# Program order from a list scheduler, first loads in 512-byte pieces, sink rows packed into 32

## The chip, the cores and the metric

The kernel runs on one core of a Trainium2 chip. The metric is the device time of one execution in microseconds (us). A core has five engines that each run their own instructions strictly in program order: PE (matrix products; its weight loads are shown as PEld), DVE (vector work), ACT (activation functions and copies), POOL (here mostly a DMA issuer that also casts in flight) and SP (issues DMAs only). Engines wait for one another by semaphores; an instruction that waits holds up everything behind it on its engine.

## The reference, cut to what matters

```python
# q, k, v: batch 4, heads 8, seq 768, head_dim 64; n_sink 4, window 128
scores = scale * q @ k.T                      # keep: is_sink | (0 <= row - col < window)
a = softmax(where(keep, scores, -1e9));  x = a @ v      # x as 3072 tokens x 512
h = x @ w_in                                  # 512 -> 2048
P = a0 + a1*h + a2*h**2 + a3*h**3
Q = 1 + |b0|*|h| + |b1|*h**2
out = (P / (Q + 1e-6)) @ w_out                # 2048 -> 512
```

Attention with a window of 128 and four sink tokens, then two matrix products with a rational function between them.

## The kernel before

The 3072 tokens are cut into 12 steps of 256 (three per batch entry). A step's attention runs per head pair i (four of them): `scores` (four products into the one buffer ps_s), `exps` on ACT, `mask` on DVE for two pairs at a time, `attend` on PE into the one buffer ps_m, `normalize` on DVE. `sink_scores` and `sink_exps` treat the sink tokens once per step; `spread_k` lays the transposed k out as block-diagonal weights. `turn_x` transposes the result: by PE for steps 0 and 1, by SP's DMA transposes afterwards.

The second half of a step m works on h as 128 partitions x 4096 columns. `project_in` makes it in four quarters (16 products each, into two buffers ps_h), `copy_in` moves a quarter to SBUF on ACT. DVE then does `magnitude` (|h|), a half of `square`, `denominator`, `even`, `odd`, `odd_h`, `numerator`; ACT does the other half of `square`, and the reciprocal of Q as `log_den` (Ln) and `recip_den` (Exp). `gate` on DVE multiplies, `project_out` (two tiles of tokens, each in two groups of eight products, one buffer ps_out) and `store` finish.

What sets the order: the program is written out by hand. A prologue does step 0's attention, then a loop over slots t (L611 ff.) issues in each slot a quarter of `project_in`, an attention pair two steps ahead, one group of `project_out`, and the element-wise work by j = t mod 4. Every engine's order follows from that. Data arrive by three ways: SP loads step 0's k, q and v as fp32, which are cast on ACT and DVE; POOL's DMAs load everything later with a cast; SP's DMA transposes turn k and q from step 2 on. POOL has eight DMAs under way at most: the ninth waits until the first has landed.

Of the kernel before, what the change touches and what calls it, by code (L numbers as in the profile page):

```python
# [17 lines left out]
def kernel(  # L18
# [62 lines left out]
    k_sink = [const_pool.tile([P, 640], BF16, name=f"k_sink_{n}") for n in range(2)]  # L81
# [12 lines left out]
    one_eps = const_pool.tile([P, 1], FP32, name="one_eps")  # L94

# [13 lines left out]

    def load_q(tile_i):  # L110
# [42 lines left out]
    def cast_v():
        for e in range(2):
            lo, hi = e * 64, (e + 1) * 64
            nc.vector.tensor_copy(out=v_bd[0][lo:hi, :, :, e, 0:D], in_=raw["v"][lo:hi])

    def load_w_in(half):
        f0, f1 = half * DF // 2, (half + 1) * DF // 2
        for c in range(NDMC):  # L160
            nc.gpsimd.dma_start(out=w_in_sb[c][:, f0:f1], in_=moe_w_in[c * P:(c + 1) * P, f0:f1])

    def load_w_out(part):
        for c in range(part * NFFC // 2, (part + 1) * NFFC // 2):
            nc.gpsimd.dma_start(out=w_out_sb[c], in_=moe_w_out[c * P:(c + 1) * P, :])
# [576 lines left out]
```

## Time and profile before

| | us |
|---|---|
| median of 3 runs (297.49 to 298.47) | 298.21 |
| profiled execution, its own time | 298.49 |
| its span, first to last instruction | 296.8 |
| DVE busy in the span | 239.3 |
| PE busy | 235.5 |
| ACT busy | 214.2 |
| POOL busy (issuing DMAs counts) | 116.1 |

How to read it: three engines are busy for more than 70% of the span, DVE most. These shares are means over stages; the windows in the rows below cut the span at the end of step 0's attention, the start of the first `gate` and the end of the last one.

### The profile page before, as it was taken

What the parts mean: (1) busy time and instruction counts of PE and PEld (TensorE: products, weight loads), DVE (VectorE), ACT (ScalarE), POOL (GpSimd) and SP (SyncE); (2) the same over time, 40 slices, a digit from 0 to 9 for tenths busy, and PEclk for the clock granted to TensorE, in tenths of its full rate; (3) what the DMA queues carried; (4) which work ended last, traced back from release to release, by engine and by line L of the source; (5) the groups of instructions that cost most, each with busy time, mean ns of one, the idle gap of its engine ahead of it and who ended that gap; (6) DMA issues with size and microseconds to landing.
All of it is one profiled execution on the core that took longest, in us unless ns stands there. A gap on an engine that the chain in (4) does not pass through costs nothing.

```text
span 296.8 us, 4876 instructions
## 1 busy us (share of the span) xinstructions
PE 235.5 (79%) x1856; PEld 167.4 (56%) x1876; DVE 239.3 (81%) x320; ACT 214.2 (72%) x201; POOL 116.1 (39%) x178
## 2 busy tenths in 40 slices
PE   0516866658609899999989899998999999997864
PEld 0414555546507777767767677676677767652321
DVE  6606623736794999999999999999999999999930
ACT  2104261684735998989979899898998989897810
POOL 8938668879091046181651793380000000000000
PEclk9999997996957999999999999999999999997999
DMA  8999999999999199398995999292110121100111
GB/s 160 127 171 80 157 127 158 142 171 201 143 114 47 29 129 128 80 136 108 116 103 105 147 107 121 27 140 63 55 41 17 53 55 53 38 35 35 71 38 72
DMA packets 116632, 28.94 MB, mean 98 GB/s; under 512 B 110464, under 2 KB 112512, under 8 KB 116608
## 3 DMA queue, kind: packets, MB, share of 16 engines
q0 software_dynamic: 72752, 12.74, 64.1%
q1 hardware_dynamic: 43856, 15.88, 26.6%
q8 instruction: 15, 0.25, 0.4%
q14 instruction: 9, 0.07, 0.1%
HBM read 27.30 MB, written 6.29 MB: 113 GB/s over the span
## 4 chain that ended last, share of the span: by engine, by line
DVE 56%; PE 16%; DMA 8%; ACT 7%; issue 6%; SPq 5%; POOL 1%; DVEq 0%; ACTq 0%; POOLq 0%
DVE sq L470 8%; DVE num L474 8%; PE ps_h L419 7%; DVE g L492 6%; DVE den L454 6%; DVE x_n L384 5%; DVE num L460 4%; DVE den L449 4%; DVE e L348 4%; PE ps_out L500 4%; DVE sq L443 3%; PE ps_o L371 3%; DMA b_bc<-in_moe_b_dram 3%; DVE sq L465 2%; ACT hb L426 2%
## 5 line engine op out<-in xcount | busy, mean ns | idle before, releaser
L419 PE MATMUL ps_h<-xblk,w_in_sb 128*128 128x256 bf16 x768 | 98.5, 284 | 8.3 <-DMA xblk<-x_n 7.5
L500 PE MATMUL ps_out<-w_out_sb,g 128*128 128x512 bf16 x364 | 87.8, 385 | 7.6 <-ACT o_t L505 4.0
L419 PEld LDWEIGHTS <-w_in_sb 128*128 128x128 bf16 x768 | 76.4, 102 | 20.5 <-DMA xblk<-x_n 7.8
L151 POOL DMA_DIRECT2D v_bd<-in_v_dram x88 | 57.3, 670 | 28.7 <-PE ps_o L371 12.2
L426 ACT ACTIVATE hb<-ps_h 128x1024 bf16<-128x1024 f32 x48 | 49.1, 1022 | 26.2 <-PE ps_h L419 26.2
L500 PEld LDWEIGHTS <-g 128*128 128x128 bf16 x384 | 37.3, 99 | 45.6 <-issue 7.0
L480 ACT ACTIVATE lnq<-den,one_eps,qsc 128x2048 f32<-128x2048 bf16 x24 | 50.4, 2098 | 10.9 <-DVE den L454 10.9
L486 ACT ACTIVATE den<-lnq 128x2048 bf16<-128x2048 f32 x24 | 46.2, 1924 | 0.0
L341 ACT ACTIVATE e<-ps_s 128x768 bf16<-128x768 f32 x48 | 38.9, 816 | 2.8 <-PE ps_s L331 2.8
L131 POOL DMA_DIRECT2D k_bf<-in_k_dram x22 | 20.3, 937 | 46.9 <-DMA kT_flat<-k_bf 46.6
L371 PE MATMUL ps_o<-v_bd,e 128*128 128x130 bf16 x352 | 31.4, 228 | 9.1 <-DVE x_n L384 4.2
L331 PE MATMUL ps_s<-qT,kT 128*128 128x192 bf16 x192 | 25.7, 260 | 14.9 <-ACT e L341 14.6
L371 PEld LDWEIGHTS <-e 128*128 128x128 bf16 x352 | 26.1, 102 | 19.4 <-DVE x_n L384 4.9
L454 DVE TENSOR_TENSOR den<-den,sq 128x2048 bf16<-128x2048 bf16 x24 | 29.0, 1215 | 0.0
L331 PEld LDWEIGHTS <-kT 128*128 128x128 bf16 x192 | 18.4, 104 | 17.7 <-issue 16.2
L474 DVE TENSOR_TENSOR num<-num,sq 128x4096 bf16<-128x4096 bf16 x12 | 27.5, 2292 | 0.4
L492 DVE TENSOR_TENSOR g<-num,den 128x4096 bf16<-128x4096 bf16 x12 | 27.4, 2284 | 0.1
L470 DVE TENSOR_TENSOR sq<-sq,hb 128x4096 bf16<-128x4096 bf16 x12 | 27.4, 2284 | 0.1
L384 DVE SCALAR_TENSOR_TENSOR x_n<-ps_o,csc,rec 128x256 bf16<-128x256 f32 x48 | 23.2, 484 | 1.7
L381 DVE RECIPROCAL rec<-ps_o 128x4 f32<-128x4 f32 x48 | 8.5, 177 | 18.7 <-PE ps_o L371 18.5
L348 DVE TENSOR_TENSOR e<-e,edge 128x1024 bf16<-128x1024 bf16 x24 | 16.4, 683 | 8.3 <-ACT e L341 8.3
L441 ACT ACTIVATE sq<-hb 128x2048 bf16<-128x2048 bf16 x12 | 22.9, 1910 | 0.0
(67 smaller groups left out, 205.8 us busy)
## 6 DMA issues: line engine op xcount, KB each, us to landing
out_dram<-o_t SPq DMA_DIRECT2D x24, 256.0 KB, 2.4
k_bf<-in_k_dram POOLq DMA_DIRECT2D x22, 128.0 KB, 5.4
v_bd<-in_v_dram POOLq DMA_DIRECT2D x88, 32.0 KB, 4.4
q_bf<-in_q_dram POOLq DMA_DIRECT2D x21, 128.0 KB, 5.9
w_in_sb<-in_moe_w_in_dram POOLq DMA_DIRECT2D x8, 256.0 KB, 7.6
w_out_sb<-in_moe_w_out_dram POOLq DMA_DIRECT2D x16, 128.0 KB, 5.0
stage_q<-in_q_dram SPq DMA_DIRECT2D x3, 256.0 KB, 5.2
xblk<-x_n SPq DMA_TRANSPOSE x40, 3.5
```

The source lines that it names most:

```text
L151: nc.gpsimd.dma_start(out=t_[lo:hi, i, :, e, 0:D], in_=src)
L331: nc.tensor.matmul(ps[:, n // 2, (n % 2) * 192:(n % 2) * 192 + 192], lhsT=kT_fix[s % 2][:, i * NHF + n, :], rhs=qT_fix[b % 2][:, i, c:c + ...
L371: nc.tensor.matmul(ps_o[:, n, :], lhsT=l_, rhs=r_.rearrange("p e c -> p (e c)"), start=(m == 0), stop=(m == len(terms) - 1))
L419: nc.tensor.matmul(ps[:, n, :], lhsT=w_in_sb[c][:, fc * P:(fc + 1) * P], rhs=xblk[m][:, c, :], start=(c == 0), stop=(c == NDMC - 1))
L426: nc.scalar.activation(out=hb[m][:, j * GW:(j + 1) * GW], in_=ps_h.pop((m, j)).rearrange("p n c -> p (n c)"), func=AF.Copy)
L454: nc.vector.tensor_tensor(out=den[m][:, c], in0=den[m][:, c], in1=sq[m][:, c], op=ALU.add)
L470: nc.vector.tensor_tensor(out=sq[m][:, c], in0=sq[m][:, c], in1=hb[m][:, c], op=ALU.mult)
L474: nc.vector.tensor_tensor(out=num[m][:, c], in0=num[m][:, c], in1=sq[m][:, c], op=ALU.add)
L480: nc.scalar.activation(out=lnq[m, part], in_=den[m][:, c], func=AF.Ln, scale=qsc, bias=one_eps)
L486: nc.scalar.activation(out=den[m][:, c], in_=lnq[m, part], func=AF.Exp, scale=-1.0)
L492: nc.vector.tensor_tensor(out=g_of[m][:, c], in0=num[m][:, c], in1=den[m][:, c], op=ALU.mult)
L500: nc.tensor.matmul(ps_out[m, tt], lhsT=g_of[m][:, co:co + P], rhs=w_out_sb[fc], start=(fc == 0), stop=(fc == NFFC - 1))
```

## The change

The hand-written prologue and slot loop go. Every unit of work becomes a piece with an engine, an assumed length, a rank and the pieces that it depends on. At build time a list scheduler goes through simulated time: whenever an engine is free it takes, of the pieces whose inputs are done and whose PSUM buffer is free, the one with the lowest rank. The order in which pieces were taken is the order in which the program is then emitted. The chip sees the same five in-order engines; the work per step is unchanged.

Beside the order: k and q of step 0 (256 tokens) are loaded with two neighbouring tokens per partition, so that a piece of memory is 512 bytes and not 256, and the casts and the copies after the transposes sort even and odd tokens again (those of q move from DVE to ACT); v of step 0 comes through POOL with the cast in flight and not through SP; the sink rows of v are loaded densely into 32 partitions and spread by DVE (once per batch entry) and not by eight small DMAs; b and a are loaded right behind k and q; and the second half of w_in is issued in front of k and q of step 1.

```diff
-    k_sink = [const_pool.tile([P, 640], BF16, name=f"k_sink_{n}") for n in range(2)]
+    KW = P + 2 * NS
+    k_sink = [const_pool.tile([P, NPB * KW], BF16, name=f"k_sink_{n}") for n in range(2)]
...
+    def load_two(dst, src):
+        nc.sync.dma_start(out=dst.rearrange("p (h t d) -> p h t d", h=H, t=2),
+                          in_=src[:, 0:2 * P, :].rearrange("h (p t) d -> p h t d", t=2))
+
+    def by_token(t_):
+        return t_.rearrange("p (h t d) -> p t h d", h=H, t=2)
...
+    def cast_k2():
+        k_bf[0] = early[:, 3:5, :]
+        nc.vector.tensor_copy(out=k_bf[0].rearrange("p t (h d) -> p t h d", h=H),
+                              in_=by_token(raw["k"]))
...
+    def load_v_sink():
+        for b in range(B):
+            nc.gpsimd.dma_start(out=stage_s[:, b, :], in_=v[b, :, 0:NS, :])
+
+    def spread_v_sink(b):
+        nc.vector.tensor_tensor(
+            out=v_sink[0:NR, b, :, 0:D], in0=stage_s[:, b:b + 1, :].to_broadcast([NR, H, D]),
+            in1=ind[0:NR].unsqueeze(2).to_broadcast([NR, H, D]), op=ALU.mult)
+        nc.vector.tensor_copy(out=v_sink[0:NR, b, :, D], in_=ind[0:NR])
...
+    def place_q2():
+        dst = qT_fix[0][:, :, 0:2 * P].rearrange("p i (c t) -> p i c t", t=2)
+        for t in range(2):
+            nc.scalar.activation(out=dst[:, :, :, t], in_=ps_q["two"][:, :, t, :], func=AF.Copy)
...
+            if s == 0:
+                for t in range(2):
+                    nc.vector.tensor_copy(
+                        out=kT[lo:hi, :, lo:hi].rearrange(
+                            "p (i n) (c t) -> p i n c t", i=NPB, t=2)[:, :, :, :, t],
+                        in_=src[lo:hi, :, t, :].rearrange("p i (n c) -> p i n c", n=NHF))
...
-    cast_k()
-    turn_k(0)
-    spread_k(0)
-    for n in range(NQ_HW):
-        cast_q(n)
-        turn_q(n)
-    sink_edge, csc, qsc, (a0, a1, a2, a3) = scalars()
-    load_w_in(0)
-    feed(1)
-    load_v(1)
-    load_w_in(1)
...
-    for t in range(NSLOT + 14):
-        p, j = divmod(t, 4)
-        in_m = p < NSTEP
-        ns = ahead_s.get(t, (t + 8,))
...
-        if j == 1:
-            if in_c:
-                log_den(c, A_)
-                denominator(c, B_)
-            if in_g:
-                gate(c - 1)
...
+    piece(("load_k2",), "SP", 0.6, -22, load_k2, kind="hw", load=2.0)
+    piece(("load_q2",), "SP", 0.6, -21, load_q2, kind="hw", load=2.0)
+    piece(("load_q", 2), "SP", 0.6, -20, lambda: load_q(2), kind="hw", load=1.4)
...
+    for half in range(2):
+        for c in range(NDMC):
+            piece(("load_w_in", half, c), "POOL", 0.55, -18.9 + half * 0.05,
+                  lambda half=half, c=c: load_w_in(half, c), kind="sw", load=1.25)
...
+    piece(("scal_in",), "SP", 1.0, -19.8, lambda: (
+        nc.sync.dma_start(out=b_bc, in_=moe_b.partition_broadcast(P)),
+        nc.sync.dma_start(out=a_bc, in_=moe_a.partition_broadcast(P))), kind="hw", load=0.2)
+    piece(("babs",), "ACT", 0.15, -12, lambda: nc.scalar.activation(out=babs, in_=b_bc, func=AF.Abs),
+          [("scal_in",)])
...
+    for b in range(B):
+        piece(("spread_vs", b), "DVE", 0.7, -18 if b == 0 else 12 * b - 13,
+              lambda b=b: spread_v_sink(b),
+              [("consts",), ("clear_vs",), ("load_vs",), ("norm", 0, NPB - 1) if b else None])
...
+            piece(("exp", m, hf), "ACT", on_act(HW), r_ + 7.2 + hf,
+                  lambda m=m, part=part: recip_den(m, part), [("ln", m, hf)])
+        piece(("even", m), "DVE", 1.27, r_ + 6.2, lambda m=m: even(m),
+              [("sq", m, 0), ("sq", m, 1), ("gate", m - 1) if m else ("cast_q",)])
...
+        piece(("gate", m), "DVE", on_dve(MW, 2), r_ + 9.3, lambda m=m: gate(m),
+              [("num", m), ("exp", m, 0), ("exp", m, 1)]
+              + ([("gemm2", m - 2, NTS - 1, 1)] if m >= 2 else
+                 [("turned_k", 0), ("turn_q2",), ("turn_q", 2)]))
...
+                able = [w for w in waiting[e]
+                        if (not w.takes or room[w.takes])
+                        and (not w.kind or lanes[w.kind][count[w.kind] % 8] <= now + 1e-9)]
+                if not able:
+                    continue
+                w = min(able, key=lambda w_: (w_.rank, w_.order))
+
+                if any(f_.eng == e and left[f_.name] == 1 and f_.rank < w.rank - HOLD_R
+                       for end, x_ in ends if end < now + HOLD_F * w.length
...
+                if w.takes:
+                    room[w.takes] -= 1
+                if w.frees:
+                    returns.append((end, w.frees))
+                ends.append((end, w))
+                done.append(w)
+            if not moved:
...
+    for w in run_list():
+        if w.run:
+            w.run()
```

Where the instructions stand now, at three places. First ACT, from the first quarters of h (hb) on; e are the exps of the pairs, lnq is `log_den`, sq is ACT's half of `square`, xblk the copy behind `turn_x`. Before:

```order
L404 ACTIVATE xblk<-ps_xT 128x512 x2
L426 ACTIVATE hb<-ps_h 128x1024 x2
L341 ACTIVATE e_1_95<-ps_s 128x4x192
L318 ACTIVATE e_sink<-ps_sink 128x256
L341 ACTIVATE e_1_95<-ps_s 128x4x192
L426 ACTIVATE hb<-ps_h 128x1024
L341 ACTIVATE e_1_97<-ps_s 128x4x192 x2
L404 ACTIVATE xblk<-ps_xT 128x512
L426 ACTIVATE hb<-ps_h 128x1024
L441 ACTIVATE sq<-hb 128x2048
```

The same place now:

```order
L437 ACTIVATE xblk<-ps_xT 128x512 x2
L462 ACTIVATE hb<-ps_h 128x1024 x2
L477 ACTIVATE sq<-hb 128x2048
L462 ACTIVATE hb<-ps_h 128x1024
L516 ACTIVATE lnq<-den,one_eps,qsc 128x2048
L375 ACTIVATE e_1_95<-ps_s 128x4x192
L347 ACTIVATE e_sink<-ps_sink 128x256
L375 ACTIVATE e_1_95<-ps_s 128x4x192
L462 ACTIVATE hb<-ps_h 128x1024
L375 ACTIVATE e_1_97<-ps_s 128x4x192
L522 ACTIVATE den<-lnq 128x2048
```

The square and the first logarithm of step 0 moved in front of step 1's first exps, and the fourth quarter of h stands in front of step 1's third exps and no longer behind all four and the first `turn_x`.

Second DVE, around a `gate` (g) in the middle of the program; num<-num,sq is `numerator`, num<-sq `even`, den<-hb `magnitude`, den<-den,sq `denominator`, rec and x_n are `normalize`, e is `mask`. Before:

```order
L474 TENSOR_TENSOR num<-num,sq 128x4096
L381 RECIPROCAL rec<-ps_o 128x4
L384 SCALAR_TENSOR_TENSOR x_n<-ps_o,csc,rec 128x2x128
L348 TENSOR_TENSOR e_1_97<-e_1_97,edge 128x16x64
L449 TENSOR_SCALAR den<-hb 128x1024
L443 TENSOR_TENSOR sq<-hb 128x2048
L454 TENSOR_TENSOR den<-den,sq 128x2048
L381 RECIPROCAL rec<-ps_o 128x4
L384 SCALAR_TENSOR_TENSOR x_n<-ps_o,csc,rec 128x2x128
L454 TENSOR_TENSOR den<-den,sq 128x2048
L492 TENSOR_TENSOR g<-num,den 128x4096
```

Now:

```order
L496 TENSOR_SCALAR num<-sq,acoef 128x4096
L501 TENSOR_SCALAR sq<-sq,acoef 128x4096
L416 RECIPROCAL rec<-ps_o 128x4
L419 SCALAR_TENSOR_TENSOR x_n<-ps_o,csc,rec 128x2x128
L506 TENSOR_TENSOR sq<-sq,hb 128x4096
L510 TENSOR_TENSOR num<-num,sq 128x4096
L416 RECIPROCAL rec<-ps_o 128x4
L419 SCALAR_TENSOR_TENSOR x_n<-ps_o,csc,rec 128x2x128
L382 TENSOR_TENSOR e_1_95<-e_1_95,edge 128x16x64
L485 TENSOR_SCALAR den<-hb 128x1024
L528 TENSOR_TENSOR g<-num,den 128x4096
L490 TENSOR_TENSOR den<-den,sq 128x2048
```

Before, the two denominators of step m+1 stood between the numerator and the gate of step m; now the gate stands in front of both. The denominator rows of step m itself stand one row (of `spread_k`) and this whole stretch ahead of its gate.

Third POOL, from its first DMAs on. Before:

```order
L206 DMA v_sink<-in_v_dram 4x4x64 x8
L161 DMA w_in_sb_105<-in_moe_w_in_dram 128x1024
L161 DMA w_in_sb_106<-in_moe_w_in_dram 128x1024
L161 DMA w_in_sb_107<-in_moe_w_in_dram 128x1024
L161 DMA w_in_sb_108<-in_moe_w_in_dram 128x1024
L131 DMA k_bf<-in_k_dram 128x8x64 x2
L118 DMA q_bf<-in_q_dram 128x8x64 x2
L151 DMA v_bd_92<-in_v_dram 64x4x64 x8
```

Now:

```order
L170 DMA v_bd_91<-in_v_dram 64x4x64 x8
L195 DMA stage_s<-in_v_dram 32x1x64 x4
L176 DMA w_in_sb_105<-in_moe_w_in_dram 128x1024
L176 DMA w_in_sb_106<-in_moe_w_in_dram 128x1024
L176 DMA w_in_sb_107<-in_moe_w_in_dram 128x1024
L176 DMA w_in_sb_108<-in_moe_w_in_dram 128x1024
L176 DMA w_in_sb_105<-in_moe_w_in_dram 128x1024
L176 DMA w_in_sb_106<-in_moe_w_in_dram 128x1024
L176 DMA w_in_sb_107<-in_moe_w_in_dram 128x1024
L176 DMA w_in_sb_108<-in_moe_w_in_dram 128x1024
L162 DMA k_bf<-in_k_dram 128x8x64 x2
L136 DMA q_bf<-in_q_dram 128x8x64 x2
```

k and q of step 1 moved behind all of w_in.

## Rows read from the trace of the kernel before

**Rows 1.** Four windows: length, busy PE, PEld, DVE, ACT, POOL; clock, DMA share, GB/s.
```profile
0.00:30.85 30.85, 10.52 (x74) 7.91 (x74) 16.83 (x50) 6.94 (x11) 22.98 (x47) 1.00 1.12 133
30.85:95.19 64.34, 41.05 (x353) 32.86 (x354) 35.97 (x66) 33.62 (x35) 42.79 (x61) 0.84 1.77 143
95.19:284.92 189.73, 176.68 (x1399) 123.60 (x1417) 186.53 (x207) 172.43 (x154) 50.33 (x71) 0.99 0.63 79
284.92:296.80 11.88, 7.24 (x32) 3.04 (x32) 0.00 (x0) 1.19 (x2) 0.00 (x0) 1.00 0.15 56
```
**Rows 2.** Timeline of the start: start, length, instruction, idle before it and releaser.
```profile
12.94 0.52 PE L331 MATMUL ps_s<-qT,kT 128*128 128x192 bf16 x2
...
21.54 0.20 ACT L234 ACTIVATE babs<-b_bc 128x2 f32<-128x2 f32 x1 [11.43 <-DMA b_bc<-in_moe_b_dram]
...
31.99 3.08 PE L419 MATMUL ps_h<-xblk,w_in_sb 128*128 128x256 bf16 x14 [0.26 <-ACT xblk L404]
...
36.47 1.91 PE L419 MATMUL ps_h<-xblk,w_in_sb 128*128 128x256 bf16 x16
```
**Rows 3.** The chain that ended last: start, length, what (a DMA to its landing).
```profile
12.22 9.29 DMA b_bc<-in_moe_b_dram
```
**Rows 4.** Groups by line on DVE in the start: count, busy, mean ns, idle.
```profile
L156 DVE CAST v_bd<-stage_kv 64x1024 bf16<-64x1024 f32 x2 | 1.4, 689 | 0.0
L293 DVE COPY kT<-ps_kT 64x1024 bf16<-64x1024 bf16 x4 | 2.7, 686 | 0.8 <-PE ps_kT L278 0.8
L263 DVE COPY qT<-ps_qT 128x512 bf16<-128x512 bf16 x5 | 2.1, 424 | 2.9 <-PE ps_qT L262 2.9
```
**Rows 5.** Timeline of POOL: issues of step 1's v, and what each waited for.
```profile
19.46 0.61 POOL L151 DMA_DIRECT2D v_bd<-in_v_dram x1 [0.72 <-DMA w_in_sb<-in_moe_w_in_dram]
21.12 0.61 POOL L151 DMA_DIRECT2D v_bd<-in_v_dram x1 [1.06 <-DMA w_in_sb<-in_moe_w_in_dram]
22.41 0.61 POOL L151 DMA_DIRECT2D v_bd<-in_v_dram x1 [0.67 <-DMA k_bf<-in_k_dram]
23.93 1.98 POOL L151 DMA_DIRECT2D v_bd<-in_v_dram x3 [0.91 <-DMA k_bf<-in_k_dram]
```
**Rows 6.** DMA issues by line: count, KB, median us to landing.
```profile
qT<-q_bf SPq DMA_TRANSPOSE x19, 3.5
v_sink<-in_v_dram POOLq DMA_DIRECT2D x8, 2.0 KB, 3.9
```
**Rows 7.** Groups by line on DVE, whole span.
```profile
L454 DVE TENSOR_TENSOR den<-den,sq 128x2048 bf16<-128x2048 bf16 x24 | 29.0, 1215 | 0.0
L474 DVE TENSOR_TENSOR num<-num,sq 128x4096 bf16<-128x4096 bf16 x12 | 27.5, 2292 | 0.4
L470 DVE TENSOR_TENSOR sq<-sq,hb 128x4096 bf16<-128x4096 bf16 x12 | 27.4, 2284 | 0.1
L384 DVE SCALAR_TENSOR_TENSOR x_n<-ps_o,csc,rec 128x256 bf16<-128x256 f32 x48 | 23.2, 484 | 1.7
L449 DVE TENSOR_SCALAR den<-hb 128x1024 uint32<-128x1024 uint32 x24 | 18.1, 754 | 0.0
L348 DVE TENSOR_TENSOR e<-e,edge 128x1024 bf16<-128x1024 bf16 x24 | 16.4, 683 | 8.3 <-ACT e L341 8.3
L460 DVE TENSOR_SCALAR num<-sq,acoef 128x4096 bf16<-128x4096 bf16 x12 | 16.1, 1344 | 0.2
```
**Rows 8.** Groups by line on ACT, whole span.
```profile
L480 ACT ACTIVATE lnq<-den,one_eps,qsc 128x2048 f32<-128x2048 bf16 x24 | 50.4, 2098 | 10.9 <-DVE den L454 10.9
L426 ACT ACTIVATE hb<-ps_h 128x1024 bf16<-128x1024 f32 x48 | 49.1, 1022 | 26.2 <-PE ps_h L419 26.2
L486 ACT ACTIVATE den<-lnq 128x2048 bf16<-128x2048 f32 x24 | 46.2, 1924 | 0.0
L341 ACT ACTIVATE e<-ps_s 128x768 bf16<-128x768 f32 x48 | 38.9, 816 | 2.8 <-PE ps_s L331 2.8
L505 ACT ACTIVATE o_t<-ps_out 128x512 f32<-128x512 f32 x24 | 14.4, 599 | 11.2 <-PE ps_out L500 11.2
```

More of the change, by code (lines that the diff above doesn't have):

```diff
@@ L153, in cast_v, with cast_q @@
[L153 to L158, printed above, removed]
-        f0, f1 = half * DF // 2, (half + 1) * DF // 2
[L160 to L165, printed above, removed]
+    def cast_q():
+        nc.scalar.activation(out=early[:, 2, :], in_=raw["q"][:, 2, :], func=AF.Copy)
@@ L251, in scalars, with turn_q2 @@
         nc.vector.tensor_tensor(out=acoef[:, 1:4], in0=a_bc[:, 1:4], in1=cpow, op=ALU.mult)
-        return sink_edge, csc, qsc, [acoef[:, n:n + 1] for n in range(4)]
+    kT_flat, ps_q, ps_x = {}, {}, {}
+    def turn_q2():
+        ps = ps_op.tile([P, 512], FP32, tag="ps_out", name="ps_qT").bitcast(BF16)
+        ps = ps.rearrange("p (i t c) -> p i t c", i=NPB, t=2)
+        for i in range(NPB):
+            for t in range(2):
+                nc.tensor.transpose(ps[:, i, t, :], early[:, t, i * P:(i + 1) * P], ident)
+        ps_q["two"] = ps
@@ L538, in do_scores @@
-    def do_scores(n):
-        s, i = divmod(n, NPB)
-        if s < NSTEP:
-            scores(s, i)
-            exps(s, i)
-    def do_mask(n):
-        s, i = divmod(n, NPB)
-        if s < NSTEP and i % 2 == 1:
-            mask(s, i // 2)
-    def do_attend(n):
-        s, i = divmod(n, NPB)
-        if s < NSTEP:
-            attend(s, i)
-    def do_norm(n):
-        s, i = divmod(n, NPB)
-        if s < NSTEP:
-            normalize(s, i)
-            if i % 2 == 1:
-                turn_x(s, i // 2)
@@ new lines, with piece, on_dve @@
+    work = {}
+    class Piece:
+        pass
+    def piece(name, eng, length, rank, run, after=(), takes=None, frees=None, lat=0.0, kind=None,
+              load=0.0):
+        w = Piece()
+        w.name, w.eng, w.length, w.rank, w.run = name, eng, length, rank, run
+        w.after = [a_ for a_ in after if a_ is not None]
+        w.takes, w.frees, w.lat, w.kind, w.load = takes, frees, lat, kind, load
+        w.order = len(work)
+        assert name not in work
+        work[name] = w
+    def on_dve(cols, rate, extra=0.0):
+        return 0.065 + extra + cols / (960.0 * rate)
@@ new lines @@
+    piece(("babs",), "ACT", 0.15, -12, lambda: nc.scalar.activation(out=babs, in_=b_bc, func=AF.Abs),
+          [("scal_in",)])
+    piece(("scalars",), "DVE", 1.7, -12, scalars, [("babs",)])
+    piece(("mask_tiles",), "DVE", 1.4, -17, mask_tiles, [("consts",)])
+    for n in range(3):
+        piece(("clear_v", n), "DVE", 1.0, (-20, -10, -4)[n], lambda n=n: zero(v_flat[n]))
+        piece(("ones", n), "DVE", 0.2, (-20, -10, -4)[n], lambda n=n: ones_columns(v_fix[n]),
+              [("clear_v", n)])
@@ new lines @@
+    for n in range(2):
+        later = [("norm", 0, NPB - 1)] if n else []
+        piece(("clear_kT", n), "DVE", 0.95, -19.9 + n * 5, lambda n=n: zero(kT_fix[n]))
+        piece(("clear_ks", n), "DVE", 0.35, -19.8 + n * 12, lambda n=n: zero(k_sink[n]), later)
+        piece(("clear_qT", n), "DVE", 0.3, -19.8 + n * 12,
+              lambda n=n: nc.vector.memset(qT_fix[n][:, :, S:S + P], 0.0), later)
+        for grp in range(2):
+            piece(("clear_e", grp, n), "DVE", 0.35, -19.7 + n * 5,
+                  lambda grp=grp, n=n: zero_gaps(e_fix[grp, n]))
```

603 lines of the change are left out of this document (326 added, 277 removed).

## The prediction, made before the changed kernel had run

> **What bounds the kernel now.** I read the windows first, cut at the end of step 0's last `normalize` (30.85), the start of the first `gate` (95.19) and the end of the last one (284.92). In the third window DVE is busy 186.5 of 189.7 us: it waits 3.2 us in all, so there DVE is the bound, with PE behind it (176.7 busy, 13.0 idle) [rows 1]. The last 11.9 us are without DVE: two `project_out` tiles, copy, store. In the first two windows DVE works only 16.8 of 30.9 and 36.0 of 64.3 us. The column adds up to 239.3 us of work; of its idle time 14.0 + 28.4 = 42.4 us lie ahead of the first gate. That is what an order can win here; 239.3 plus the tail is what it can't pass.
>
> Then the timeline, for what those 42.4 us wait for. In the start, ACT's first exps stand behind `babs`, which needs b; b is issued at 12.22 behind eight loads of v and lands 9.29 later [rows 3], so ACT idles 11.43 and goes on at 21.54 [rows 2], though the first scores ran at 12.94. In the second window PE is busy 41 us, ACT 34 and DVE 36 of 64, at a granted clock of 0.84 [rows 1]: none is full, they wait for each other in turn, since the slots mix quarters of h with attention of steps 1 to 3 in one fixed order.
>
> **The start, part by part.** b now goes out as SP's fourth load, some 8 us earlier. The exps then hang on q: its casts, transposes and copies take the same time as before, moved from DVE to ACT, and the first scores stay at about 13. So exps begin at about 13.3 instead of 21.7. From there to the last `normalize` it took 9.2 us before; that gives 22.5. DVE's own list gives nearly the same: POOL issues eight v and four sink loads (0.6 us each, from 3.6 on) until 11, the sink rows land 3.9 later [rows 6], and behind the spread that waits for them stand two clears, two masks and four `normalize`: 22.8. I take 22.8, 8 us earlier. Bounds: 20 (the sink rows in time, all clears hidden) to 31 (nothing won).
>
> [...]
>
> Work added or removed on DVE: the cast of v goes (2 x 0.69), three copies of q go to ACT (3 x 0.42), the spread of step 0's k is four strided copies instead of two of 0.69 [rows 4]. No row shows a copy with step 2; below lies half a row each (0.34), above the fp32 rate of `normalize` (0.484 for 256 elements, 0.97 for 512 [rows 7]); I take the 0.42 of the other PSUM copy, 1.7 in all, and keep 1.4 to 3.9. The four spreads of sink rows (512 elements each on 32 partitions) lie between 0.34 and 1.1, I take 0.75, 3.0 in all. Sum: -1.4 - 1.3 + 0.3 + 3.0 = +0.7, so 240.0 us of DVE work; -1 to +4 with the bounds.
>
> [...]
>
> The 512-byte loads and the wider casts save at most the wait for k and q, and DVE is still at its clears then: 0, bounds -1.5 to +1 (the strided casts at up to twice 0.84).
>
> **The fill, from 22.8 to the first gate.** `turn_x` and its copy as before: 31.99 - 30.85 = 1.1 [rows 2], so the first quarter of h starts at 23.9; 3.1 and 1.9 us for two quarters [rows 2], one copy of 1.0 [rows 8]: 29.9. DVE has only the other three spreads and two clears there.
>
> k and q of step 1 now stand behind all of w_in. Tiles of w_in landed 1.66 us apart, tiles of k 1.5 [rows 5]. Eight from 11.5 on: 25.5; four of k and q: 31.5. Before, they had landed by about 25 but were first used behind the first quarter of h, after 32, so this costs little: PE turns k at 29.7, q 4 at 33.
>
> ACT then has, from 29.9, the square (as long as an Exp, 1.9), the third copy once its quarter is there (34.0), the first logarithm 2.1, two exps of 0.82 and the small sink one [rows 8]: the first mask of step 1 at 38.1. From that mask to the gate DVE has 4 masks, 2 `magnitude`, 7 `normalize` (0.18 + 0.48), one square and one denominator, 2 spreads, `even` and `odd`, `odd_h`, `numerator`: 2.7 + 1.5 + 4.6 + 2.4 + 1.9 + 2.7 + 2.3 + 2.3 = 20.4 us [rows 4, 7]. One wait inside: PE does the third `attend` of step 1 behind the first scores of step 2, which need q 6. That lands behind eight v (0.61 each) and four tiles of 1.5: 42.9, plus a transpose of 1.2 + 3.5 [rows 6] = 47.6; DVE wants that `attend` at 44.8 and gets it at 49.3: 4.5 us. So the first gate starts at 38.1 + 20.4 + 4.5 = 63.0. Bounds: 55 (no such wait, w_in faster) to 80 (the fill's 28.4 us of idle time unchanged).
>
> **From the first gate to the end.** At that gate the new order has done less: before, 52.8 us of DVE work lay ahead of it. Of that the new order still has to do four `normalize` (2.6), two masks (1.4), a spread and a sink mask (1.0), one `magnitude`, one square and two denominators of step 1 (4.4): 9.4. With the +0.7 that is 44.1 us done, 195.9 left. Idle time in the rest: I keep 3.2, since DVE's work per step is the same and PE has the same share of it (176.7 plus some 9 us for two more quarters and four more pairs, in 199 us: 93%, as before). Tail 11.9, the same instructions.
>
> Sum: 63.0 + 195.9 + 3.2 + 11.9 = 274.0 us of span. The profiled execution took 1.7 us more than its span (298.49 against 296.8) and the median of the runs lay 0.3 below it: 275.4 us.
>
> **The rivals.** *The loads set the fill.* For it: the DMA share is 1.77 in the second window, and w_in's second half, some 7 us, now goes ahead of step 1. If the fill keeps its idle time: 240.0 + (42.4 - 8) + 3.2 + 11.9 = 289.5, 290.9 us measured. Against it: before, the waits there are mostly of engine for engine.
>
> *PE and DVE hold each other up in the steady part.* ps_m and ps_s are single, PE has 7% to spare, and the order comes from assumed lengths. One us more per step and 11 steps: 286.4. Against: units as long as now and no new dependence.
>
> *Slower.* Place: the gate. Before, it stands behind the next step's two denominators, nearly a step after its own. Now only `even`, `odd`, `odd_h`, `numerator`, two `normalize`, a mask and a `magnitude` lie between the second denominator and its gate: 2.7 + 2.3 + 2.3 + 1.3 + 0.7 + 0.75 = 10.0 us [rows 7]. In that time ACT must do Ln 2.1 and Exp 1.9 and what is queued between them; the longest such list of the new order has a copy of h, a sink exp, an exp, a square and an output copy: 1.0 + 0.3 + 0.8 + 1.9 + 0.6, in all 8.6 [rows 8]. The margin is 1.4. It decides once ACT's list, waits for PE included, exceeds 10.0 + 2.1 at each of 11 gates: 11 x 2.1 = 23 us eat the gain. At 2.5 each: 302.9 us.
>
> *Tighter.* q 6 in time and k 1 earlier: 63.0 becomes 56, 268.4 us.
>
> **How the numbers follow.** Forecast 0.58, own range 270 to 282 (waits in the fill from none of the 4.5 to another 6). Loads 0.13 at 291, PE and DVE 0.12 at 286, tighter 0.11 at 268, slower or nothing gained 0.06. The range that holds 8 in 10 reaches from 265 to 289. Differences below 0.3% can't be told from no change; faster 0.94, same 0.02, slower 0.04.
>
> **What would show it.** In the changed profile: `babs` before 11 with no long wait; the last `normalize` of step 0 near 23; first quarter of h near 24; first gate near 63; DVE about 98% busy from there to 12 us before the end; no wait of the gate for ACT's Exp. Wrong if the first gate comes after 75, if DVE's idle time behind it exceeds 10 us, or if its work is off 240 by over 4.

## The result, and the profile after

The changed kernel takes 283.81 us (median of 4 runs, 281.89 to 284.91) against 298.26 of the kernel before: a ratio of 0.951, 95% interval 0.945 to 0.957. It is 14.4 us faster; 22.8 were forecast. The profiled execution took 284.91 us with a span of 283.2, against 274.0 predicted. Here and below a time is the median of all executions of a kernel, while its ratio to the kernel before, with the interval, is that of its fast executions, so small differences are read from the ratios.

Four windows of the changed kernel, cut at the same events as [rows 1] (last `normalize` of step 0, start of the first `gate`, end of the last one); the columns are those of [rows 1]:

```profile
0.00:21.36 21.36, 9.00 (x74) 7.55 (x74) 17.51 (x55) 8.77 (x13) 17.00 (x38) 0.92 0.89 136
21.36:62.99 41.63, 30.54 (x245) 24.26 (x246) 26.15 (x47) 25.73 (x25) 31.21 (x46) 0.75 1.65 129
62.99:269.68 206.69, 185.01 (x1505) 131.30 (x1522) 197.57 (x224) 180.73 (x162) 77.13 (x99) 1.00 0.95 95
269.68:283.20 13.52, 8.14 (x37) 3.32 (x34) 0.06 (x1) 1.79 (x3) 0.00 (x0) 1.00 0.16 59
```

Read them in pairs with [rows 1]. DVE's idle time ahead of the first gate is 3.9 + 15.5 = 19.3 us; before it was 42.4. That is the whole gain and more: 23.1 us less. On the other side stand DVE's idle time behind that gate (206.69 - 197.57 = 9.1 us, before 3.2), the tail (13.5, before 11.9) and the work itself (241.3, before 239.3): 5.9 + 1.6 + 2.0 = 9.5 us. 23.1 - 9.5 is the 13.6 us between the two spans.

The start and the fill, from the timelines of ACT, DVE and PE (start, length, instruction, idle time before it):

```profile
9.42 0.20 ACT L608 ACTIVATE babs<-b_bc 128x2 f32<-128x2 f32 x1 [0.30 <-DMA b_bc<-in_moe_b_dram]
...
12.67 0.81 ACT L375 ACTIVATE e<-ps_s 128x768 bf16<-128x768 f32 x1 [0.57 <-PE ps_s L365]
...
20.88 0.48 DVE L419 SCALAR_TENSOR_TENSOR x_n<-ps_o,csc,rec 128x256 bf16<-128x256 f32 x1
...
28.17 0.69 DVE L485 TENSOR_SCALAR den<-hb 128x1024 uint32<-128x1024 uint32 x1 [4.27 <-ACT hb L462]
...
37.46 0.69 DVE L382 TENSOR_TENSOR e<-e,edge 128x1024 bf16<-128x1024 bf16 x1 [4.48 <-ACT e L375]
...
57.98 0.86 DVE L322 COPY kT<-kT_flat 64x1024 bf16<-64x1024 bf16 x2 [3.79 <-DMA kT_flat<-k_bf]
...
62.99 2.27 DVE L528 TENSOR_TENSOR g<-num,den 128x4096 bf16<-128x4096 bf16 x1
```

`babs` no longer waits for b (11.43 us in [rows 2], now 0.30), step 0 ends at 21.4, and the first gate starts at 62.99. Three waits of some 4 us are left in the fill.

Behind the first gate, the waits of DVE and of PE (engine and line, what they waited for: us in total, times, longest), and DVE's copies of the transposed k:

```profile
DVE den L485 <- ACT hb L462: 4.9, 4, 2.5
DVE g L528 <- ACT den L522: 1.4, 1, 1.4
...
PE ps_h L455 <- DMA xblk<-x_n: 5.2, 3, 3.4
PE ps_sink L337 <- DVE x_n L419: 4.4, 4, 1.7
PE ps_out L536 <- ACT o_t L541: 4.4, 6, 1.6
...
L322 DVE COPY kT<-kT_flat 64x1024 bf16<-64x1024 bf16 x20 | 10.6, 532 | 5.1 <-DMA kT_flat<-k_bf 4.9
```

The second `magnitude` waits for ACT's copy of h. One of the four times, on both engines:

```profile
200.64 2.28 DVE L528 TENSOR_TENSOR g<-num,den 128x4096 bf16<-128x4096 bf16 x1
202.85 1.22 DVE L490 TENSOR_TENSOR den<-den,sq 128x2048 bf16<-128x2048 bf16 x1
...
204.10 2.09 ACT L516 ACTIVATE lnq<-den,one_eps,qsc 128x2048 f32<-128x2048 bf16 x1 [2.94 <-DVE den L490]
...
206.10 1.00 ACT L462 ACTIVATE hb<-ps_h 128x1024 bf16<-128x1024 f32 x1
...
207.13 0.69 DVE L485 TENSOR_SCALAR den<-hb 128x1024 uint32<-128x1024 uint32 x1 [2.46 <-ACT hb L462]
```

The gate stands ahead of the next step's first denominator, the logarithm waits for that denominator, the copy stands behind the logarithm on ACT, and DVE waits for the copy. From this I made theory A: move the gate behind the denominator, and the two waits of this form (3.9 of the 4.9 us) go. PE's 5.2 us for the transposed x suggested another: the loads, which take a larger share there than before (DMA share 0.95 against 0.63).

### The profile page after: what moved, and what is told of

Same layout as the page of the kernel before. It is cut to its first block, busy times and chain, and to the rows that moved or that the text cites. A ratio compares the mean times of both kernels' runs of the same rounds, so it can differ in the third digit from the quotient of the medians.

```text
span 283.2 us, 4847 instructions
## 1 busy us (share of the span) xinstructions
PE 232.7 (82%) x1857; PEld 166.4 (59%) x1876; DVE 241.3 (85%) x323; ACT 217.0 (77%) x203; POOL 125.3 (44%) x182
## 4 chain that ended last, share of the span: by engine, by line
DVE 51%; DMA 19%; ACT 8%; PE 8%; issue 8%; POOL 5%; SPq 1%; DVEq 0%; ACTq 0%; POOLq 0%
DVE num L510 7%; DVE den L490 7%; DVE sq L506 6%; DMA w_out_sb<-in_moe_w_out_dram 5%; PE ps_out L536 5%; DVE x_n L419 5%; DVE sq L501 4%; DVE num L496 4%; DVE den L485 4%; DVE e L382 4%; DMA q_bf<-in_q_dram 3%; DVE sq L479 3%; DVE g L528 3%; DMA k_bf<-in_k_dram 3%; DMA w_in_sb<-in_moe_w_in_dram 3%
## 5 line engine op out<-in xcount | busy, mean ns | idle before, releaser
L455 PE MATMUL ps_h<-xblk,w_in_sb 128*128 128x256 bf16 x768 | 94.2, 276 | 5.4 <-DMA xblk<-x_n 5.2
L170 POOL DMA_DIRECT2D v_bd<-in_v_dram x96 | 65.6, 704 | 42.7 <-PE ps_o L406 30.3
L455 PEld LDWEIGHTS <-w_in_sb 128*128 128x128 bf16 x768 | 74.6, 99 | 16.6 <-DMA xblk<-x_n 6.0
L462 ACT ACTIVATE hb<-ps_h 128x1024 bf16<-128x1024 f32 x48 | 49.2, 1029 | 22.8 <-PE ps_h L455 22.7
L406 PE MATMUL ps_o<-v_bd,e 128*128 128x130 bf16 x352 | 33.0, 234 | 11.1 <-DVE x_n L419 7.8
L365 PE MATMUL ps_s<-qT,kT 128*128 128x192 bf16 x192 | 26.3, 265 | 4.4 <-ACT e L375 2.0
L162 POOL DMA_DIRECT2D k_bf<-in_k_dram x22 | 21.1, 968 | 13.7 <-DMA kT_flat<-k_bf 9.4
L541 ACT ACTIVATE o_t<-ps_out 128x512 f32<-128x512 f32 x24 | 14.6, 609 | 14.1 <-PE ps_out L536 14.1
L485 DVE TENSOR_SCALAR den<-hb 128x1024 uint32<-128x1024 uint32 x24 | 17.2, 715 | 9.5 <-ACT hb L462 9.4
```

Source lines behind the costliest of these rows:

```text
L170: nc.gpsimd.dma_start(out=v_bd[s][e * 64:(e + 1) * 64, i, :, e, 0:D], in_=v[b, h, g * TS:(g + 1) * TS, :].rearrange("(j p) d -> p j d", p=64))
L365: nc.tensor.matmul(ps[:, n // 2, (n % 2) * 192:(n % 2) * 192 + 192], lhsT=kT_fix[s % 2][:, i * NHF + n, :], rhs=qT_fix[b % 2][:, i, c:c + ...
L406: nc.tensor.matmul(ps_o[:, n, :], lhsT=l_, rhs=r_.rearrange("p e c -> p (e c)"), start=(m == 0), stop=(m == len(terms) - 1))
L455: nc.tensor.matmul(ps[:, n, :], lhsT=w_in_sb[c][:, fc * P:(fc + 1) * P], rhs=xblk[m][:, c, :], start=(c == 0), stop=(c == NDMC - 1))
L462: nc.scalar.activation(out=hb[m][:, j * GW:(j + 1) * GW], in_=ps_h.pop((m, j)).rearrange("p n c -> p (n c)"), func=AF.Copy)
```

## The experiments

Below, "first to last gate" is the time between the starts of the first and the last `gate` in the profiled execution, from a row like these (form: count, ns of one min/median/max, first and last start). Before, changed, large pieces, less DVE work, less DVE and PE work:

```profile
L492 DVE TENSOR_TENSOR g<-num,den x12: 2281/2284/2292, 95.2 to 282.6; 128x4096 bf16<-128x4096 bf16 x12
...
L528 DVE TENSOR_TENSOR g<-num,den x12: 2273/2284/2293, 63.0 to 267.4; 128x4096 bf16<-128x4096 bf16 x12
...
L529 DVE TENSOR_TENSOR g<-num,den x12: 2283/2285/2293, 58.1 to 262.8; 128x4096 bf16<-128x4096 bf16 x12
...
L528 DVE TENSOR_TENSOR g<-num,den x12: 2271/2284/2292, 59.7 to 262.7; 128x4096 bf16<-128x4096 bf16 x12
...
L528 DVE TENSOR_TENSOR g<-num,den x12: 2282/2286/2294, 59.5 to 261.5; 128x4096 bf16<-128x4096 bf16 x12
```

### The gate's place (den_first)

```diff
-    for w in run_list():
+    done = run_list()
+    for m in range(NSTEP - 1):
+        names = [w.name for w in done]
+        g_, d_ = names.index(("gate", m)), names.index(("den", m + 1, 0))
+        if g_ < d_:
+            done.insert(d_, done.pop(g_))
+    for w in done:
```

> The changed kernel with one thing moved: on DVE each step's gate stands behind the next step's first denominator instead of ahead of it; the other engines' orders stay. Theory A (idle time of DVE behind the first gate comes from that place: the denominator waits behind the 2.3 us gate, ACT's next logarithm waits for the denominator, the copy of h behind it comes late and the second magnitude on DVE waits for it): the 3.9 us of those waits go and nothing else changes, 283.8 becomes about 279.9, 278.5 to 281.5, and the logarithm no longer waits for the denominator (7.1 us before). Theory B (PE and its single PSUM buffers set the pace there): DVE's waits only move to other places, 283 or more.

283.32 us, ratio 0.950 [0.946, 0.953]: no measurable gain. The waits did what theory A says: those of `magnitude` went from 4.9 to 1.2 us, the logarithm's from 7.1 to 1.9. From the fifth gate to the ninth the time fell too; changed kernel, this run, kernel before:

```profile
143.27:221.82 78.55, 73.41 (x621) 53.45 (x628) 73.75 (x90) 70.52 (x66) 17.05 (x24) 1.00 0.33 57
...
146.17:221.24 75.07, 72.11 (x624) 52.91 (x623) 72.42 (x90) 69.67 (x64) 16.18 (x24) 1.00 0.31 53
...
170.51:244.10 73.59, 71.25 (x596) 51.74 (x604) 72.38 (x89) 68.29 (x64) 17.97 (x25) 1.00 0.52 69
```

That is 3.5 us less, most of the way to the kernel before, whose gate stands behind both denominators of the next step. But new waits came, 6.1 us of DVE for `attend`, and DVE's idle time behind the first gate is 11.5 us. The largest, 3.7 us, comes from here (timeline of PE in the changed kernel and in this run, and a window of this run in the columns of [rows 1]):

```profile
132.30 1.70 PE L455 MATMUL ps_h<-xblk,w_in_sb 128*128 128x256 bf16 x14 [3.38 <-DMA xblk<-x_n]
...
131.23 3.17 PE L455 MATMUL ps_h<-xblk,w_in_sb 128*128 128x256 bf16 x14 [4.45 <-DMA xblk<-x_n]
...
130.00:135.00 5.00, 3.77 (x16) 2.41 (x17) 4.09 (x5) 1.06 (x2) 4.25 (x6) 0.51 2.35 166
```

PE waits 4.45 us for the transposed x of step 5, and the 14 products behind it take 3.17 us where they took 1.70 in the changed kernel: the granted clock was 0.51 in that window (the last row), and 1.00 from 130 to 135 us in the changed kernel. So A describes these waits rightly and is worth 3.5 us in the later steps; the whole gets no shorter, since the wait for x takes as much ahead of them.

### Less work for DVE, for PE, for both, for DVE and ACT (dve_less, pe_less, dve_pe_less, dve_act_less)

```diff
-        piece(("odd_h", m), "DVE", on_dve(MW, 2), r_ + 7.5, lambda m=m: odd_h(m), [("odd", m)])
+        piece(("odd_h", m), "DVE", on_dve(MW, 2), r_ + 7.5, lambda m=m: odd_h(m, A_), [("odd", m)])
```
```diff
         for fc in range(f0, f1):
+            if fc in (1, 9):
+                continue
```
```diff
-            nc.scalar.activation(out=den[m][:, c], in_=lnq[m, part], func=AF.Exp, scale=-1.0)
+            n = MW // 4 if part == (0, 2) else MW // 2
+            nc.scalar.activation(out=den[m][:, c.start:c.start + n], in_=lnq[m, part][:, 0:n],
+                                 func=AF.Exp, scale=-1.0)
```

> The changed kernel, with odd_h done on half of its columns in every step (that half of odd_h is left out): some 13.7 us less work for DVE in the same order, PE and ACT untouched. Theory A (DVE sets the pace behind the first gate): 11 to 13.7 us less, 270 to 273. Theory B (PE is as much the bound as DVE): most of the work taken away comes back as waits of DVE, 279 or more, since PE already has 185.0 of 206.7 us there and the rest are waits for its buffers.

281.51 us, ratio 0.943 [0.939, 0.947]: B's number. DVE's work fell by 12.1 us to 229.2, and of that 2.3 us arrived, an amount for which the intervals of the two kernels still overlap.

> The changed kernel, with 14 instead of 16 products for each output tile (two of the sixteen slices of the hidden dimension are left out of project_out): some 10 us less work for PE in the same order, DVE and ACT untouched. Theory A (DVE sets the pace, PE only waits): only the tail gets shorter, about 1.3 us, 282.5. Theory B (PE holds DVE up in the steady part): 5 us less or more, 275 to 279.

283.00 us, ratio 0.945 [0.940, 0.950]: A's number, with 1.8 us less by the ratio (first to last gate 204.9 us, against 204.4). So neither theory holds in both runs: more is in play than one engine that sets the pace.

> The changed kernel with both reductions of the runs before: odd_h on half of its columns, and 14 of 16 products per output tile (both halves are left out of the result). Alone, 13.7 us less DVE work brought 2.3 us and 10 us less PE work 0.8. Theory B2 (PE is the next bound right behind DVE: either alone only lets the other one set the pace): together 8 to 12 us less, 272 to 276. Theory E (neither is; the third thing, ACT's list with its waits or the transposes, holds both): 279 or more.

279.89 us, ratio 0.937 [0.932, 0.941]: E, not B2. Between 150 and 225 us, where the DMA share is 0.30 to 0.33 against 2.06 from 95 to 140 us in the changed kernel (rows: changed kernel, less DVE work, less of both):

```profile
150.00:225.00 75.00, 69.86 (x588) 50.97 (x595) 71.42 (x86) 68.79 (x65) 15.33 (x22) 1.00 0.30 53
...
150.00:225.00 75.00, 71.93 (x614) 52.36 (x612) 68.75 (x88) 69.78 (x66) 13.88 (x20) 1.00 0.30 52
...
150.00:225.00 75.00, 68.59 (x588) 50.47 (x595) 69.17 (x88) 70.10 (x67) 14.47 (x20) 1.00 0.33 53
```

With both cut, no engine is over 94% busy, yet the pace hardly rises: from the fifth gate to the ninth it takes 76.7 us (77.2 with less DVE work alone, 78.3 with less PE work alone, 78.6 in the changed kernel).

> The run with half of odd_h once more, and now ACT has less to do as well: the first of the two Exp of each step works on half of its columns (half of odd_h and a quarter of the reciprocal are left out of the result); some 0.9 us less for ACT in each of 12 steps, all orders stay. With odd_h alone 13.7 us less DVE work brought 2.3 us (281.5), and with PE's 10 us less on top 279.9; between 150 and 225 us ACT was then busy 70 of 75 us, PE 68.6, DVE 69.2. Theory G (ACT is the next bound right behind DVE): 277 or less. Theory H (no single engine is; the waits run round through PE, ACT and DVE by the fixed orders): 279 to 281.5.

280.70 us, ratio 0.939 [0.934, 0.943]: H, not G. So taking some 10 us from one engine, or from two, brings 1 to 4 us; DVE's 95.6% behind the first gate (197.57 of 206.69 us) was not a bound of its own. The same window of this run:

```profile
150.00:225.00 75.00, 72.44 (x624) 53.28 (x622) 68.64 (x89) 68.43 (x66) 15.33 (x23) 1.00 0.32 54
```

Here PE is 96.6% busy; with DVE and PE relieved it is ACT that is busiest, at 93.5%. So two readings are left: waits that run round through the three engines by their fixed orders, or three lists of nearly equal length, of which the one left uncut takes over. No run took work from all three. Against equal lists as the whole story stands den_first: with the work unchanged and only the gate moved, the four steps from the fifth gate on take 75.1 us, less than in any run with work taken away (76.2 in this one).

### The loads (big_pieces, x5_first)

```diff
-            in_=k[b, :, r0:r0 + P, :].rearrange("h p d -> p h d"))
+            in_=k[b].rearrange("h s d -> (h s) d").rearrange("(r h) d -> r h d", h=H)[r0:r0 + P])
```
(the same for q; of the second run SP's order is shown behind it)

> The changed kernel, in which each 128-token load of k and q from step 1 on reads one stretch of 2 KB per partition instead of eight of 256 bytes (other numbers of the same tensors are loaded, so the attention is that of other data; bytes, targets and all orders stay). Theory C (what the earlier loads cost: while they run, the DMA transposes land in 6 us instead of 3.6, PE waits 5.2 us behind the first gate for the transposed x, and DVE 3.8 us ahead of it for the transposed k of step 3): both waits go, and the first gate comes 3 to 4 us earlier; 277 to 281. Theory D (DVE's own order sets the pace and these waits are slack): 283 or more behind a gate at 62 to 63.

278.89 us, ratio 0.933 [0.928, 0.938]. The size is C's and the place half so: the first gate comes at 58.1, 4.9 us earlier, and that is the whole gain; DVE's wait for step 3's k is gone. First to last gate it takes 204.7 us as against 204.4, and PE's wait for x stays (5.5 us, longest 4.4). So the loads' small pieces cost 3 to 5 us in the fill (other profiles of the unchanged fill have the first gate at 60.9 to 63.0); behind it two differences cancel, 2.9 us less from the first gate to the fourth and 3.2 more from there to the fifth, where that wait lies. DVE's work fell too, 241.3 to 238.5, part of it in the copies of k (mean 452 ns, above 532, in the kernel before 418).

```diff
+L443 DMA_TRANSPOSE xblk<-x_n 128x2x128 x2
 L304 DMA_TRANSPOSE kT_flat<-k_bf 128x4x128 x2
-L287 DMA_TRANSPOSE qT_103<-q_bf 128x4x128
-L443 DMA_TRANSPOSE xblk<-x_n 128x2x128 x2
-L287 DMA_TRANSPOSE qT_103<-q_bf 128x4x128
+L287 DMA_TRANSPOSE qT_103<-q_bf 128x4x128 x2
```

> The changed kernel with one change on SP: the last two transposes of step 5's x stand ahead of the two of k and the one of q that stood in front of them; nothing else moves. These are the ones for which PE waited 3.4 us at 132 (4.5 in the run with the denominator first, 4.4 in the run with large pieces). Theory F (transposes land in the order of SP's queue, so the three in front make x late): PE's wait there falls below 1 us; the time falls by up to 3 us, 281 to 283. Rival (they land late because loads of POOL run beside them, wherever they stand): a wait of 3 us or more stays, 283.8.

283.19 us, ratio 0.948 [0.944, 0.953]. PE does not wait for x at all between 105 and 140 us, as F says. The time from issue to landing of all transposes of x between 95 and 140 us, changed kernel and this one:

```profile
DMA to landing us min/median/max: 4.4/6.8/7.8
...
DMA to landing us min/median/max: 3.6/4.2/6.4
```

The two that were moved took 7.2 and 7.5 us and now take 4.1 and 4.2; but the pairs ahead of them and behind them, which were not moved, fell as well (from 7.6 and 7.7 to 5.4 and 6.4, from 6.1 and 7.8 to 3.6 and 3.7), so SP's queue is not shown to be the whole reason. And first to last gate stays at 204.9 us: in the changed kernel a wait of 3.4 us of PE taken away is worth nothing that could be measured.

In other runs it is another matter. PE at the same place with less DVE work, with less DVE and PE work, and with large pieces:

```profile
129.68 3.00 PE L455 MATMUL ps_h<-xblk,w_in_sb 128*128 128x256 bf16 x14 [4.49 <-DMA xblk<-x_n]
...
128.09 3.17 PE L455 MATMUL ps_h<-xblk,w_in_sb 128*128 128x256 bf16 x14 [3.61 <-DMA xblk<-x_n]
...
125.67 3.17 PE L456 MATMUL ps_h<-xblk,w_in_sb 128*128 128x256 bf16 x14 [4.42 <-DMA xblk<-x_n]
```

Here, in den_first and in dve_act_less the wait is 3.6 to 5.4 us, the 14 products behind it take 3.00 to 3.17 us in the rows above and in den_first (1.70 in the changed kernel), DVE then waits 2.5 to 5.3 us for `attend`, and the fourth gate to the fifth takes 21.0 to 23.3 us; in the changed kernel, pe_less, x5_first and tail_two it takes 18.9 to 19.2 (20.3 in small_pieces, with a wait of 3.0). So each of these edits loses part of what it wins at this one place. How much they would bring without it was tried for den_first alone (den_x5_tail, below).

### The tail (tail_two), and all three edits (den_x5_tail)

```diff
-            ps_out[m, tt] = ps_op.tile(
-                [P, DM], FP32, tag="ps_out", name="ps_out")
+            alt = m >= 10 and tt == 1
+            ps_out[m, tt] = (ps_mp if alt else ps_op).tile(
+                [P, DM], FP32, tag="ps_m" if alt else "ps_out", name="ps_out")
```

> The changed kernel, with the second output tile of the last two steps in the other PSUM buffer (the one of attend, idle by then), so that its products need not wait for the copy of the first tile; all orders stay. Theory A (the tail's extra 1.6 us against before are PE's wait for the single output buffer, some 0.7 us for each tile): 1.5 to 2.3 us less, about 281.7. Rival (the tail is PE's products alone and starts with the last gate): 283.8 unchanged.

281.36 us, ratio 0.942 [0.937, 0.947]: theory A. From the last gate's start (265.3) to the end of the span 13.3 us against 15.8. PE in the changed kernel, and then here:

```profile
266.98 3.61 PE L536 MATMUL ps_out<-w_out_sb,g 128*128 128x512 bf16 x15 [0.69 <-ACT o_t L541]
...
271.33 3.61 PE L536 MATMUL ps_out<-w_out_sb,g 128*128 128x512 bf16 x16 [0.73 <-ACT o_t L541]
...
275.68 3.61 PE L536 MATMUL ps_out<-w_out_sb,g 128*128 128x512 bf16 x16 [0.73 <-ACT o_t L541]
...
261.78 12.90 PE L537 MATMUL ps_out<-w_out_sb,g 128*128 128x512 bf16 x58
```

In the changed kernel step 10's second tile is still running when the last gate ends at 269.7, and each tile then waits 0.7 us for the copy of the one ahead. With a second buffer PE runs through.

> Three edits together on the changed kernel: each gate behind the next step's first denominator, the two transposes of step 5's x ahead of k and q on SP, the last two steps' second output tile in the other PSUM buffer. With the denominator first, four steps behind the fifth gate took 75.1 us instead of 78.6, but the wait for x before it had eaten that. If theory A is right on the steady part and F on the transposes: 3.5 us from the first two and 2 from the tail, 278.5, 277 to 280. If not: 281, the tail alone.

280.37 us, ratio 0.938 [0.933, 0.943]: clear of the changed kernel's interval and the better version that came out, but not told apart from tail_two alone. The 2 us are the tail's; of the 3.5 in the steady part at most 1 came. In the profile the four steps behind the fifth gate take 75.1 us again and the fourth gate to the fifth 18.9, but the first gate to the fourth takes 64.0 us (61.1 in the changed kernel, 61.0 to 62.0 in pe_less, x5_first, tail_two and den_first): there the gain is lost, and why is not shown.

### The start alone, in the order written by hand (before_b, before_bv), and the pieces (small_pieces)

```diff
+    nc.sync.dma_start(out=b_bc, in_=moe_b.partition_broadcast(P))
+    nc.sync.dma_start(out=a_bc, in_=moe_a.partition_broadcast(P))
     load_v(0)
-    nc.sync.dma_start(out=b_bc, in_=moe_b.partition_broadcast(P))
-    nc.sync.dma_start(out=a_bc, in_=moe_a.partition_broadcast(P))
```

> The kernel before with one thing changed: b and a are loaded ahead of step 0's eight loads of v, on the same queue; the order written by hand stays. Theory A (the start is passed on in full, whatever the order behind it): the 11.4 us that ACT waits for b shrink to about 3, and the end comes 8 us earlier: 290, 289 to 292. Rival (the fill's waits take it up, and it is the scheduler's order that makes the early start worth something): 295 to 298.

297.88 us, ratio 0.9985 [0.996, 1.001]: nothing. ACT's exps start at 14.6 instead of 21.7, and then DVE waits for v:

```profile
21.12 1.41 DVE L156 CAST v_bd<-stage_kv 64x1024 bf16<-64x1024 f32 x2 [4.75 <-DMA stage_kv<-in_v_dram]
```

In the kernel before, the last load of v landed 10.8 us after its issue, at about the same time as b, but [rows 2] name only b, which was waited for first.

```diff
-            if s == 0:
-                nc.sync.dma_start(out=raw["v"][lo:hi, i], in_=src)
-            else:
-                nc.gpsimd.dma_start(out=t_[lo:hi, i, :, e, 0:D], in_=src)
+            nc.gpsimd.dma_start(out=t_[lo:hi, i, :, e, 0:D], in_=src)
...
-    cast_v()
```
(and `load_v(0)` ahead of the sink rows)

> The kernel before with the whole of the new start except for the order: b and a are loaded early as in the run before_b, and step 0's v comes through POOL with a cast in flight, ahead of the loads of the sink rows, so that neither SP's eight loads nor the two casts on DVE stand ahead of the attention; the order written by hand stays. In before_b, v landed at 21.1 us and took the place of b. Theory A (with both gone, step 0's attention ends some 6 us earlier and the hand-written order passes it on): 291 to 293. Rival (the fill of the hand-written order takes up an earlier start, whatever it is): 296 to 298.

301.57 us, ratio 1.013 [1.009, 1.016]: slower, which neither expected. The last `normalize` of step 0 starts at 20.84, as in the changed kernel; the first gate, though, at 98.1, later than the 95.2 of before:

```profile
20.84 0.48 DVE L381 SCALAR_TENSOR_TENSOR x_n<-ps_o,csc,rec 128x256 bf16<-128x256 f32 x1
...
40.75 1.02 ACT L423 ACTIVATE hb<-ps_h 128x1024 bf16<-128x1024 f32 x1 [7.29 <-PE ps_h L416]
...
98.09 2.29 DVE L489 TENSOR_TENSOR g<-num,den 128x4096 bf16<-128x4096 bf16 x1
```

A start that is 9.5 us earlier brought nothing here, but this run doesn't test the start alone. With v on POOL all of POOL's other loads come later: w_in's first tile is issued at 13.7 instead of 8.6, the k behind w_out at 75.1 instead of 70.4. PE waits for both:

```profile
35.27 0.40 PE L416 MATMUL ps_h<-xblk,w_in_sb 128*128 128x256 bf16 x1 [2.56 <-DMA w_in_sb<-in_moe_w_in_dram]
...
92.45 3.12 PE L416 MATMUL ps_h<-xblk,w_in_sb 128*128 128x256 bf16 x14 [11.87 <-DMA xblk<-x_n]
```

Waits for w_in are 5.9 us in all, none in the kernel before; the wait for the transposed x of step 2, which stands on SP behind the transposes of that k, is 11.9 us, before 7.5. These two are 10.3 us of waiting more than before, against 12.4 us lost (9.5 of the start, 2.9 at the gate). Whether the hand-written order would pass the early start on with its loads in time is not shown.

```diff
-        nc.sync.dma_start(out=dst.rearrange("p (h t d) -> p h t d", h=H, t=2),
-                          in_=src[:, 0:2 * P, :].rearrange("h (p t) d -> p h t d", t=2))
+        for t in range(2):
+            nc.sync.dma_start(
+                out=dst.rearrange("p (h t d) -> p h t d", h=H, t=2)[:, :, t, :],
+                in_=src[:, 0:2 * P, :].rearrange("h (p t) d -> p h t d", t=2)[:, :, t, :])
```

> The changed kernel, with step 0's k and q loaded in pieces of 256 bytes again (two loads each instead of one, into the same layout); casts, copies and orders stay. Theory A (DVE's clears hide the difference, as the prediction said): 283.3 to 284.5. Rival (the larger pieces bring step 0 forward): 285 to 286.

284.76 us, ratio 0.956 [0.951, 0.961]: between the two, and not told apart from the changed kernel. The start ends at 21.9 instead of 21.4 us, so half a microsecond at most is shown.

## Why the prediction was right, and where it fell short

**The start.** Right, 21.4 against 22.8: `babs` at 9.4 (forecast: before 11), exps at 12.7 (13.3). That b would land in time for this was the author's assumption: [rows 3] have it 9.29 us after its issue, behind the loads of v. In the changed kernel b, issued at 3.44 us behind three loads, landed 6.0 us later. Incomplete in its reason: the prediction let the exps hang on q and did not say that v was equally late (before_b); the change had moved both.

**The fill.** Right, 62.99 against 63.0, and its parts with it: DVE's work ahead of the gate 43.7 (44.1), waits of 4.3, 4.5 and 3.8 (by the prediction's times some 4.3 and 4.0, and the 4.5 that it names). The agreement to 0.1 us is luck: other profiles of the same fill have the gate at 60.9 to 62.5; the third wait stands elsewhere than forecast, for step 3's k and not for q 6; and the prediction's own rows give less for it, 24.8 for the eight tiles of w_in (11.5 + 8 x 1.66, not 25.5) and then 41.7 for q 6 (not 42.9), a wait of 3.3 and a gate at 61.8. big_pieces shows the cause of the wait for k, the loads in small pieces.

That start and fill add up is not a property of the start: before_bv has the same start and no gain, since its loads came later. That the early start pays here because the new order has other work ready behind it is argued, not shown: order, loads and start changed together, and how much of the 23 us each of them would win alone was not tried.

**DVE's work.** 241.3 against 240.0, by terms that offset one another. The four step-2 copies of k took 2.7 us (1.7 taken; the upper bound, 3.9, priced them like `normalize`, 0.97 each, and they took 0.71). The spreads of the sink rows with their small cast took 3.3 (3.0). The later copies of k took 2.2 more than before (mean 532 ns, before 418), for which the prediction has no term; `magnitude` and the copy of the mask's edges took 1.4 less. Why the copies took longer is not shown: in the changed kernel they take 582 ns between 40 and 95 us, where loads run (DMA share 1.89), and 418 behind 150, but in the kernel before they take 418 beside loads too (40 to 95 us, 1.69).

**Idle time behind the first gate, the step that failed.** "I keep 3.2, since DVE's work per step is the same and PE has the same share of it": measured 9.1 us, 5.9 more, two thirds of the miss of 9.2 us in the span (DVE 95.6% busy there, not 98). What the prediction left out is what the gate's new place does to the next step. It asked only whether the gate would wait for ACT's Exp, which it did once, for 1.4 us. But the gate now holds up the next denominator, with it ACT's logarithm and the copy of h behind that, and so DVE's second `magnitude`. The runs show the size: from the fifth gate to the ninth DVE idles 4.8 us against 1.2 before, 3.6 of the 5.9, and with the gate moved back behind the denominator these four steps take 75.1 us instead of 78.6, in two runs (den_first, den_x5_tail); the kernel before takes 73.6. That the whole gets no faster by it (283.3) comes from the wait for step 5's x in the first of these runs; in the second it is open. The rest of the 5.9 has no shown cause.

The rival "PE and DVE hold each other up" forecast 286.4, nearer to the 283.8 than the forecast's 275.4, and 283.8 lies outside the forecast's own 270 to 282, inside its wide 265 to 289. Its mechanism is not what was found: of the 9.1 us, DVE's waits for ACT are 6.3 and it waits for PE nowhere by name. Single edits that take away a named wait or some 10 us of one engine's work bring 0.4 to 2.4 us by their ratios, two together 4.3 at most, and part of that is lost again at step 5's x.

**The tail.** "11.9, the same instructions": 13.5. The same instructions, but PE reaches the last gate with a tile still to do; tail_two gives 2.4 us back.

## What to carry to other kernels

An earlier arrival is worth what the order and the loads behind it can use: try it alone before counting it, and see that the trial does not move other loads. When an instruction moves on one engine, follow what stands behind it there, and who waits for that, around to the engine itself. When three engines are about 90% busy, a wait by name is no price; take it away and look at the distance between two fixed events (here the gates), stretch by stretch, since a gain in one can be lost in the next. And price the last stage by what the neighbouring engine has still to do when it begins, not by its instructions.

## What the runs showed of the hardware

- In the changed kernel a transpose of x by DMA landed 2.4 us (median) after its issue between 150 and 240 us (DMA share 0.28) and 6.8 between 95 and 140 us (2.06). In x5_first two that were put ahead of three others on their queue went from 7.2 and 7.5 to 4.1 and 4.2, in a run where others that were not moved landed sooner as well.
- A DVE copy in SBUF of the same form took 418, 452 or 532 ns on average in three kernels that differ in their loads (before, big_pieces, changed), and 479 to 534 in five other runs with the loads of the third (den_first, x5_first, tail_two, dve_less, den_x5_tail).
- After a wait of 3.38 us PE's next 14 products took 1.70 us (granted clock 1.00 from 130 to 135 us in the changed kernel), after one of 4.45 us 3.17 (0.51 in den_first), after one of 3.61 us 3.17 (0.50 from 128 to 133 us in dve_pe_less). The wait's length alone does not decide: at 59.7 us in the changed kernel four products of `attend` behind a wait of 3.04 us took 0.61 us, at 63.3 four of the same form 0.39 (granted clock 0.66 from 58 to 63 us).
- In the changed kernel a DVE copy of 512 bf16 elements from PSUM with step 2 took 713 ns, one of 1024 elements with step 1 688.
